# A Sinkhorn-sorted attention with a bilinear feed-forward: k and v of later batches mixed with tokens on partitions, and two edits to the start

## The chip, the cores and the metric

The kernel runs on one core of one Trainium2 chip. The metric is the device time of one execution in microseconds. The kernel before takes 245.79 us in the median of 14 runs (245.52 to 246.59).

## The reference, cut to what matters

Inputs are q, k and v of 4 batches, 8 heads, 768 tokens and 64 elements a head, an 8 x 8 matrix per head (sort_net), and the weights w_a, w_b (512 x 1536) and w_out (1536 x 512).

```python
for _ in range(5):                      # Sinkhorn
    P = exp(P - max(P, -1)); P = P / sum(P, -1); P = P / sum(P, -2)
k_sorted = einsum('bhij,bhjcd->bhicd', P, k_b)   # blocks of 96 tokens mixed by P
v_sorted = einsum('bhij,bhjcd->bhicd', P, v_b)
attn = softmax(scale * q_b @ k_sorted.T)         # within each of the 8 blocks
x = (attn @ v_sorted), heads side by side        # 3072 x 512
out = ((x @ w_a) * (x @ w_b)) @ w_out
```

## The kernel before, in words

**Tiling.** Heads are taken in pairs: 16 pairs, numbered g, four to a batch. A token's place in a tile is p * 6 + c: partition p holds six neighbouring tokens, c from 0 to 5. With 16 partitions to a block, mixing the blocks by P is one matmul with s_all, a 128 x 128 matrix per head that holds P spread over such groups of 16 (`spread`, L153). A pair's mixed k is kept as kT (64 elements of both heads on partitions, tokens along the row), its mixed v as vT in the same manner and, turned, as vs with tokens on partitions; both in three buffers (NBUF).

**Attention of a pair.** `stage_mix` (L274) makes, for k and then v, 12 matmuls of 128 columns whose weights are 64 columns wide (6 c by 2 heads), and ACT or ACT with DVE copies the result from PSUM in the order of kT or vT. For v a transpose on SP's DMA queue (L292) makes vs from vT, but for pair 4, where `turn_v` does it on TensorE. `turn_q` (L255) or `pair_q` and `stage_q` (L244, L250: a copy on Pool and a transpose on SP) make qT. `stage_scores` (L295) makes two PSUM tiles of scores, and ACT's Exp makes eT. `stage_o` (L310, through `one_o`, L226) multiplies eT by vs, and DVE divides by the row sums into xp; `to_xT` (L316) turns xp into xT by a transpose on SP's queue. The first batch does the same in two halves of four blocks with `half_mix`, `half_scores`, `half_v`, `half_o` and `half_x` (L172 to L224), all turning on TensorE.

**Feed-forward.** `ffn_ab` (L340) takes one of 12 slices of 128 hidden columns and one half of a batch's 768 tokens: four matmuls of 384 columns by w_a and four by w_b (`ab_mms`, L330), a copy by ACT (a_sb, L352) and a product by DVE into hT (L353). `ffn_out` (L368) multiplies hT by w_out in six output tiles, each in two steps of six matmuls, and `store` copies and writes one tile.

**What sets the order.** TensorE, Pool and SP run in the order of the program text; ACT and DVE do in the start (L400 to L494), and after that a scheduler places them. The start holds the Sinkhorn chain on DVE and ACT, with unused matmuls on TensorE beside it (`keep_busy`, L166; L407 and L427), then the first half of batch 0's attention. Five feed-forward tiles are begun there without their last matmul (L488 to L494), which needs x of pair 3. Then attention work is cut in units and put between feed-forward steps: `interleave` (L562) runs the second half of batch 0 with its own steps, and `paced` (L571) spreads the 12 units of batch b + 1 (`units_full`, L531) over the steps of batch b. A unit is the mix of a pair (c_), its scores (s_), or its output with to_xT (o_). c_ of pair g also copies one element of kT on Pool (gate, L540), so that Pool issues the loads of pair g + 2 (L541) after k has been mixed. Loads run on Pool's queue and change float32 to bf16. PSUM has four single banks (psF) and two double ones (psA); mix, scores and o share psA.

Of the kernel before, what the change touches and what calls it, by code (L numbers as in the profile page):

```python
# [9 lines left out]
FP32 = mybir.dt.float32  # L10
BF16 = mybir.dt.bfloat16
# [11 lines left out]
def kernel(  # L23
# [11 lines left out]
    nc = tc.nc  # L35
    P = 128
# [129 lines left out]
    def keep_busy(ps, n, cols=512):  # L166
        for _ in range(n):
            nc.tensor.matmul(ps[:, 0:cols], lhsT=warm[:, 0:P], rhs=warm[:, 0:cols],  # L168
                             start=True, stop=True)
# [33 lines left out]
    def half_v(h, hp):  # L203
        g = h * HP + hp
        vT, vs = vTs[g % NBUF], vss[g % NBUF]
        vs_ps = psF.tile([P, NBH, 2, D], BF16, tag="F", name="vs_ps")
        for i in range(NBH):
            nc.tensor.matmul(vs_ps[:, i], lhsT=vT[:, i], rhs=ident, is_transpose=True)  # L208
        nc.vector.tensor_copy(out=vs[0:BLK, 0:NBH, V0:V0 + P],
                              in_=vs_ps[0:BLK].rearrange("p i e d -> p i (e d)"))  # L210
# [7 lines left out]
    def half_x(h, hp, eng):  # L218
        xT, xp = xT_of(0), st["x", h, hp]
        xt_ps = psF.tile([P, NBH, BLK], BF16, tag="F", name="xt_ps")  # L220
        for i in range(NBH):
            nc.tensor.matmul(xt_ps[:, i, :], lhsT=xp[:, i],  # L222
                             rhs=ident[0:BLK, 0:BLK], is_transpose=True)
        copy(eng, xT[:, hp, h * HW:(h + 1) * HW].rearrange("p (i t) -> p i t", i=NBH), xt_ps)  # L224
# [25 lines left out]
    def stage_q(g):  # L250
        qT = qtp.tile([P, NCH, P], BF16, tag="qTf", name="qTf", bufs=4)
        nc.sync.dma_start_transpose(out=qT, in_=st[g, "qc"].rearrange("p c e d -> p (c e d)"))
        st[g, "qT"] = qT
# [20 lines left out]
    def stage_mix(g, what, engines):  # L274
        src2 = loaded[g][0 if what == "k" else 1]
        to = (kTs if what == "k" else vTs)[g % NBUF]
        pitch, whole = (BLK, S + PAD) if what == "k" else (P, NB * P)
        mix = psA.tile([P, 2, 512], FP32, tag="A", name="mix")
        for c in range(NCH):
            for e in range(2):  # L280
                nc.tensor.matmul(  # L281
                    mix[e * D:(e + 1) * D, c // 3, c % 3 * P:(c % 3 + 1) * P],
                    lhsT=src2[:, e, c * D:(c + 1) * D],
                    rhs=s_all[:, 2 * g + e], start=True, stop=True)
        for hf, eng in enumerate(engines):
            n = 2 // len(engines)
            for u in range(n):
                d1 = _ap(to, (hf + u) * 3 * CG, [[whole, P], [CG, 3], [pitch, NB], [1, CG]])
                s1 = _ap(mix, (hf + u) * 512, [[1024, P], [P, 3], [CG, NB], [1, CG]])
                copy(eng, d1, s1)  # L290
        if what == "v" and g > HP:
            nc.sync.dma_start_transpose(out=vss[g % NBUF][:, :, V0:V0 + P],  # L292
                                        in_=to.rearrange("p i t -> p (i t)"))

    def stage_scores(g):  # L295
        kT, qT, eT = kTs[g % NBUF], st[g, "qT"], eTs[g % NBUF]
# [33 lines left out]
    def ab_mms(pf, w_sb, b, m, t, kcs):  # L330
        for kc in kcs:
            nc.tensor.matmul(pf[:, 0:HW], lhsT=w_sb[:, kc, m * P:(m + 1) * P],  # L332
                             rhs=x_cols(b, kc, t), start=(kc == 0), stop=(kc == KA - 1))

    def hT_of(b):
        if b not in hTs:
            hTs[b] = ffp.tile([P, KO, S], BF16, tag="hT", name="hT")
        return hTs[b]

    def ffn_ab(b, m, t, begun=()):  # L340
# [58 lines left out]
    with tc.manual_schedule(engines={ET.PE, ET.Pool, ET.SP}):  # L399
        with tc.manual_schedule(engines={ET.Activation, ET.DVE}):  # L400
# [3 lines left out]
            p_rep = const.tile([BH, NB * NB, CG // 2], FP32, name="p_rep")  # L404
            pc_ps = psA.tile([P, NB, BH], FP32, tag="A", name="pc_ps")
            heat = psA.tile([P, 2, 512], FP32, tag="A", name="heat")
            keep_busy(heat[:, 0], 8)  # L407
            for it in range(5):
                nc.scalar.activation(out=p_nat, in_=p_nat, func=AF.Exp)
                if it == 2:  # L410
                    turn_q(0, "act")
                if it == 3:
                    turn_q(1, "act")
                if it == 4:
                    turn_q(2, "act")
                    turn_q(3, "act")
                if it == 2:
                    with nc.allow_low_precision("sum of one one and zeros"):
                        nc.vector.reduce_sum(
                            out=mask, in_=_ap(ident, 0, [[P, P], [1, CG], [CG, NB]]),  # L420
                            axis=AX.X)
                nc.vector.reduce_sum(out=rsum, in_=p_nat, axis=AX.X)
                nc.vector.reciprocal(out=rsum, in_=rsum)
                if it > 0:
                    nc.tensor.matmul(heat[0:NB, 1, 0:NB], lhsT=rsum, rhs=rsum,
                                     start=True, stop=True)
                    keep_busy(heat[:, 0], (0, 4, 3, 2, 4)[it])  # L427
                nc.vector.tensor_mul(out=p_nat, in0=p_nat,
                                     in1=_ap(rsum, 0, [[NB, BH], [1, NB], [0, NB]]))
                nc.vector.reduce_sum(out=csum, in_=p_nat.transpose([0, 2, 1]), axis=AX.X)  # L430
                nc.vector.reciprocal(out=csum, in_=csum)
                if it < 4:
                    nc.vector.tensor_mul(out=p_nat, in0=p_nat,
                                         in1=_ap(csum, 0, [[NB, BH], [0, NB], [1, NB]]))
                else:
                    nc.vector.tensor_mul(
                        out=p_fin.bitcast(BF16).rearrange("h (i j u) -> h i j u", i=NB, j=NB),
                        in0=_ap(p_nat, 0, [[NB * NB, BH], [NB, NB], [1, NB], [0, 2]]),
                        in1=_ap(csum, 0, [[NB, BH], [0, NB], [1, NB], [0, 2]]))
# [43 lines left out]
            half_o(0, 2)  # L483
            half_scores(0, 3)
            half_v(0, 3)
            half_x(0, 2, "act")
            half_o(0, 3)
            begun = [psF.tile([P, 512], FP32, tag="F", name="pf") for _ in range(3)]  # L488
            begun += [psA.tile([P, 2, 512], FP32, tag="A", name="two")[:, 0] for _ in range(2)]
            for n, (m, w_sb) in enumerate(((0, w_a_sb), (0, w_b_sb), (1, w_a_sb),  # L490
                                           (1, w_b_sb), (2, w_a_sb))):
                if n == 3:
                    half_x(0, 3, "act")
                ab_mms(begun[n], w_sb, 0, m, 0, range(KA - 1))  # L494


        for c in range(4, 6):
# [30 lines left out]
            us.append(lambda: half_x(1, HP - 1, "dve"))  # L528
            return us

        def units_full(b):  # L531
            g0, us = b * HP, []

            def c_(g):
                if g < 2 * HP - 2:
                    turn_q(g)
                stage_mix(g, "k", ("act",))
                stage_mix(g, "v", ("dve", "act"))
                if 2 * HP - 2 <= g < B * HP - 2:
                    nc.gpsimd.tensor_copy(out=gate, in_=kTs[g % NBUF][0:1, 0:1])  # L540
                    load_pair((g + 2) // HP, (g + 2) % HP)  # L541

            def s_(g):
                stage_scores(g)
                if g == HP:
                    turn_v(g)
                if g in (HP, HP + 1):
                    stage_q(g + 2)
                if 2 * HP <= g + 1 < B * HP:
                    pair_q(g + 1)  # L550
                    stage_q(g + 1)

            def o_(g):
                stage_o(g)
                to_xT(g)

            for u, n in ((c_, 0), (s_, 0), (c_, 1), (s_, 1), (c_, 2), (o_, 0), (s_, 2), (c_, 3),
                         (o_, 1), (s_, 3), (o_, 2), (o_, 3)):
                us.append(lambda u=u, g=g0 + n: u(g))
            return us  # L560

        def interleave(steps, units, spare, slow=0):  # L562
            n, done = len(steps), 0
# [4 lines left out]
                    units[done]()  # L568
                    done += 1

        def paced(ab, po, units, spare):  # L571
            steps = ab + po
            total = len(steps) - 2 * spare
            done = 0
            for now, step in enumerate(steps, 1):
                step()
                while done < len(units) and done * total < now * len(units):
                    units[done]()
                    done += 1

        steps = [lambda: ffn_ab(0, 0, 0, begun[0:2]), lambda: ffn_ab(0, 1, 0, begun[2:4]),
                 lambda: ffn_ab(0, 2, 0, begun[4:5])]
# [3 lines left out]
        for b in range(B):  # L586
            ab = [lambda m=m, t=t, b=b: ffn_ab(b, m, t)
                  for m in range(KO) for t in range(2) if b > 0 or t == 1]
            po = [f for c in range(NCH) for f in ffn_out(b, c)]
            paced(ab, po, units_full(b + 1) if b + 1 < B else [], 3 if b == 0 else 2)  # L590


# [28 lines left out]
```

The softmax here doesn't subtract the row's maximum and nothing guards it: scores larger than these inputs give would overflow.

## Time and profile before

| what | value |
|---|---|
| median of 14 runs | 245.79 us (245.52 to 246.59) |
| the profiled execution | 246.59 us, of which its span is 244.8 us |
| granted TensorE clock | 1.0 over the span, from 7.3 us on |
| TensorE, weight loads, DVE, ACT, Pool busy | 97%, 56%, 45%, 43%, 25% |
| DMA packets | 53929, 28.02 MB |
| share of 16 DMA engines, Pool's queue and SP's | 40.9% and 29.4% |
| transposes on SP's queue | 33: vs 11, xT 12, qTf 10 |

An engine's share is its busy time over the span. The page cuts the span in 40 slices of 6.1 us, and each digit is a busy share in tenths:

```
PE   7898999999999999999999999999999999999994
DMA  5999999987999659995783449926223310000132
```

A row of the timeline has the start and the busy time of one or of several equal instructions, in us; what stood idle before it and what ended that is in brackets. A matmul's end is modelled, so distances from start to start are the ones to read. A DMA has its issue on its queue, and its landing, which is when the last of its 16 parts is done.

### The profile page before, as it was taken

What the parts mean: (1) busy time and instruction counts of PE and PEld (TensorE: products, weight loads), DVE (VectorE), ACT (ScalarE), POOL (GpSimd) and SP (SyncE); (2) the same over time, 40 slices, a digit from 0 to 9 for tenths busy, and PEclk for the clock granted to TensorE, in tenths of its full rate; (3) what the DMA queues carried; (4) which work ended last, traced back from release to release, by engine and by line L of the source; (5) the groups of instructions that cost most, each with busy time, mean ns of one, the idle gap of its engine ahead of it and who ended that gap; (6) DMA issues with size and microseconds to landing.
All of it is one profiled execution on the core that took longest, in us unless ns stands there. A gap on an engine that the chain in (4) does not pass through costs nothing.

```text
span 244.8 us, 5499 instructions
## 1 busy us (share of the span) xinstructions
PE 237.8 (97%) x2246; PEld 137.2 (56%) x2246; DVE 109.2 (45%) x258; ACT 104.5 (43%) x204; POOL 61.4 (25%) x88
## 2 busy tenths in 40 slices
PE   7898999999999999999999999999999999999994
PEld 2475666566645466666654466666654466565442
DVE  6675466554536144464625134454525244444110
ACT  3664764566630065646440065646430133333001
POOL 8876478612240033250500053110000000000000
PEclk9999999999999999999999999999999999999999
DMA  5999999987999659995783449926223310000132
GB/s 80 201 199 197 198 199 201 203 115 78 159 129 220 137 99 132 160 138 81 109 141 118 120 94 125 168 46 67 43 79 118 117 46 0 0 3 1 43 129 86
DMA packets 53929, 28.02 MB, mean 114 GB/s; under 512 B 30736, under 2 KB 50960, under 8 KB 53904
## 3 DMA queue, kind: packets, MB, share of 16 engines
q0 software_dynamic: 20944, 14.16, 40.9%
q1 hardware_dynamic: 32816, 13.45, 29.4%
q8 instruction: 17, 0.28, 0.5%
q14 instruction: 8, 0.07, 0.1%
q10 hardware_dynamic: 144, 0.07, 0.1%
HBM read 28.32 MB, written 6.29 MB: 141 GB/s over the span
## 4 chain that ended last, share of the span: by engine, by line
PE 94%; DVE 3%; ACT 1%; issue 1%
PE pf L332 51%; PE po L377 24%; PE mix L281 4%; PE o_ps L231 3%; PE sc L302 2%; PE heat L168 2%; PE mixh L180 2%; PE po L362 1%; PE vs_ps L208 1%; PE sc L195 1%; PE xt_ps L222 1%; PE q_ps L260 1%; PE two L332 1%; DVE xp L237 1%; DVE o_sb L164 0%
## 5 line engine op out<-in xcount | busy, mean ns | idle before, releaser
L353 DVE TENSOR_TENSOR hT<-a_sb,pf 128x384 bf16<-128x384 bf16 x95 | 52.6, 554 | 73.8 <-PE pf L332 46.4
L332 PE MATMUL pf<-xT,w_a_sb 128*128 128x384 bf16 x380 | 77.9, 326 | 0.0
L332 PE MATMUL pf<-xT,w_b_sb 128*128 128x384 bf16 x380 | 77.5, 326 | 0.0
L352 ACT CAST a_sb<-pf 128x384 bf16<-128x384 f32 x95 | 45.5, 479 | 60.9 <-PE pf L332 41.3
L377 PE MATMUL po<-w_out_sb,hT 128*128 128x512 bf16 x276 | 61.9, 379 | 0.0
L332 PEld LDWEIGHTS <-w_b_sb 128*128 128x128 bf16 x384 | 37.5, 98 | 24.6
L332 PEld LDWEIGHTS <-w_a_sb 128*128 128x128 bf16 x384 | 34.9, 98 | 22.3
L377 PEld LDWEIGHTS <-hT 128*128 128x128 bf16 x276 | 26.3, 98 | 30.0
L162 ACT COPY o_sb<-po 128x512 f32<-128x512 f32 (+1 forms) x13 | 7.5, 578 | 46.8 <-PE po L377 45.2
L164 DVE COPY o_sb<-po 128x512 f32<-128x512 f32 (+1 forms) x12 | 7.9, 656 | 35.2 <-PE po L377 26.3
L307 ACT ACTIVATE eT<-sc 96x768 bf16<-96x768 f32 x24 | 18.1, 802 | 6.8 <-PE sc L302 6.8
L540 POOL COPY gate<-kT 1x1 bf16<-1x1 bf16 x8 | 1.4, 180 | 76.1 <-ACT kT L162 76.1
L237 DVE TENSOR_TENSOR xp<-o_ps,rec 96x512 bf16<-96x512 f32 x24 | 15.9, 684 | 0.6 <-DVE rec L235 0.2
L162 ACT CAST kT<-mix 128x384 bf16<-128x384 f32 x24 | 10.3, 482 | 7.9 <-PE mix L281 7.9
L95 POOL DMA_DIRECT2D k<-in_k_dram x16 | 11.6, 722 | 5.1 <-PE pf L332 2.3
L95 POOL DMA_DIRECT2D v<-in_v_dram x16 | 11.5, 719 | 2.6 <-DMA w_b_sb<-in_moe_w_b_dram 0.9
L231 PEld LDWEIGHTS <-eT 96*128 96x128 bf16 x256 | 10.3, 97 | 3.1 <-DVE xp L237 0.6
L235 DVE RECIPROCAL rec<-o_ps 96x8 f32<-96x8 f32 x32 | 5.6, 189 | 13.8 <-PE o_ps L231 13.8
L231 PE MATMUL o_ps<-vs,eT 96*128 96x65 bf16 x256 | 11.3, 193 | 0.2 <-DVE xp L237 0.2
L246 POOL COPY qc<-q 128x768 bf16<-128x768 bf16 x10 | 8.4, 837 | 8.1 <-DMA q<-in_q_dram 8.1
L168 PE MATMUL heat<-warm 128*128 128x512 bf16 x21 | 7.9, 523 | 1.3 <-DVE warm L77 1.3
L95 POOL DMA_DIRECT2D q<-in_q_dram x12 | 8.6, 718 | 1.4 <-DMA w_b_sb<-in_moe_w_b_dram 0.6
(80 smaller groups left out, 154.5 us busy)
## 6 DMA issues: line engine op xcount, KB each, us to landing
out_dram<-o_sb SPq DMA_DIRECT2D x17, 256.0 KB, 2.0
k<-in_k_dram POOLq DMA_DIRECT2D x16, 192.0 KB, 5.4
v<-in_v_dram POOLq DMA_DIRECT2D x16, 192.0 KB, 7.0
q<-in_q_dram POOLq DMA_DIRECT2D x12, 192.0 KB, 7.1
w_a_sb<-in_moe_w_a_dram POOLq DMA_DIRECT2D x6, 256.0 KB, 10.1
w_b_sb<-in_moe_w_b_dram POOLq DMA_DIRECT2D x6, 256.0 KB, 10.5
w_out_sb<-in_moe_w_out_dram POOLq DMA_DIRECT2D x3, 512.0 KB, 12.1
out_dram<-o_sb SPq DMA_DIRECT2D x12, 128.0 KB, 2.7
```

Source lines behind the costliest of these rows:

```text
L95: nc.gpsimd.dma_start(out=to, in_=_ap(t, base, [[W, P], [S * D, 2], [1, W]]))
L162: nc.scalar.copy(out=out, in_=in_)
L168: nc.tensor.matmul(ps[:, 0:cols], lhsT=warm[:, 0:P], rhs=warm[:, 0:cols], start=True, stop=True)
L231: nc.tensor.matmul(o_ps[:, e, i * (D + 1):(i + 1) * (D + 1)], lhsT=eT[:, hf, e, i * BLK:i * BLK + P], rhs=vs[0:BLK, i0 + i, V0 - 1 + e * ( ...
L237: nc.vector.tensor_tensor(out=_ap(xp, i0 * 2 * D, [[nxp * 2 * D, BLK], [D, 2], [2 * D, NBH], [1, D]]), in0=_ap(o_ps, 1, [[1024, BLK], [511 ...
L246: nc.gpsimd.tensor_copy(out=qc.rearrange("p c e d -> p e c d"), in_=loaded[g][2].rearrange("p e (c d) -> p e c d", c=NCH))
L281: nc.tensor.matmul(mix[e * D:(e + 1) * D, c // 3, c % 3 * P:(c % 3 + 1) * P], lhsT=src2[:, e, c * D:(c + 1) * D], rhs=s_all[:, 2 * g + e], ...
L307: nc.scalar.activation(out=eT[:, hf, :, 0:HB], in_=sc[0:BLK, :, 0:HB], func=AF.Exp, scale=float(scale))
L332: nc.tensor.matmul(pf[:, 0:HW], lhsT=w_sb[:, kc, m * P:(m + 1) * P], rhs=x_cols(b, kc, t), start=(kc == 0), stop=(kc == KA - 1))
L352: nc.scalar.copy(out=a_sb, in_=pf[:, 0:HW])
L353: nc.vector.tensor_mul(out=hT[:, m, t * HW:(t + 1) * HW], in0=a_sb, in1=ab[1][:, 0:HW])
L377: nc.tensor.matmul(held["po"], lhsT=hTs[b][:, m, c * P:(c + 1) * P], rhs=w_out_sb[:, m, :], start=(m == 0), stop=(m == KO - 1))
```

## The change

It has these parts.
- The unused matmuls of the Sinkhorn chain are 128 columns wide, four for each one of 512.
- The first feed-forward tile is begun earlier: its first two matmuls stand between half_v(0, 3) and half_x(0, 2).
- Pairs 5 to 15 mix k and v in `stage_kv`: s_all is the weights and k or v the moving operand, 384 columns, so mixed tokens stand on partitions (nat). ACT, or DVE and ACT, copies it, a transpose on SP turns it (turned), and `order_kv` copies it on Pool to kT and vT in block order. `return_v` then issues the transpose from vT to vs that stage_mix issued before.
- The units' order is written out in `plan`. order_kv stands one unit after the mix and return_v two; the loads of pair g + 2 stand one unit after the mix, or three if g is 8 or 12, and without the gate copy. pair_q and stage_q move to the mix unit. Mixes of pairs 9 and 13 are done a batch earlier than before, ahead of the last step of the batch (`last`), and that of pair 8 moves into batch 0.
- hT has one buffer in place of two.

```diff
+    def stage_kv(g):
+        for n, (what, engines) in enumerate((("k", ("act",)), ("v", ("dve", "act")))):
+            src2 = loaded[g][n]
+            mix = psA.tile([P, 2, 512], FP32, tag="A", name="mix")
+            for e in range(2):
+                nc.tensor.matmul(mix[:, e, 0:W], lhsT=s_all[:, 2 * g + e], rhs=src2[:, e],
+                                 start=True, stop=True)
+            nat = att.tile([P, NCH, 2, D], BF16, tag="nat", name="nat")
+            step = 2 // len(engines)
+            for u, eng in enumerate(engines):
+                copy(eng, nat[:, :, u * step:(u + 1) * step].rearrange("p c e d -> p e c d"),
+                     mix[:, u * step:(u + 1) * step, 0:W].rearrange("p e (c d) -> p e c d", c=NCH))
+            turned = att.tile([P, NCH, P], BF16, tag="turned", name="turned")
+            nc.sync.dma_start_transpose(out=turned, in_=nat.rearrange("p c e d -> p (c e d)"))
+            st[g, what, "nat"], st[g, what] = nat, turned
+
+    def order_kv(g):
+        for what, to in (("k", kTs[g % NBUF][:, 0:S].rearrange("p (i c t) -> p c i t", i=NB, c=NCH)),
+                         ("v", vTs[g % NBUF][:, :, 0:BLK].rearrange("p i (c t) -> p c i t", c=NCH))):
+            nc.gpsimd.tensor_copy(out=to, in_=st[g, what].rearrange("p c (i t) -> p c i t", i=NB))
+
+    def return_v(g):
+        nc.sync.dma_start_transpose(out=vss[g % NBUF][:, :, V0:V0 + P],
+                                    in_=vTs[g % NBUF].rearrange("p i t -> p (i t)"))
...
-            hTs[b] = ffp.tile([P, KO, S], BF16, tag="hT", name="hT")
+            hTs[b] = ffp.tile([P, KO, S], BF16, tag="hT", name="hT", bufs=1)
...
-            keep_busy(heat[:, 0], 8)
+            keep_busy(heat[:, 0], 32, P)
...
-                    keep_busy(heat[:, 0], (0, 4, 3, 2, 4)[it])
+                    keep_busy(heat[:, 0], (0, 16, 12, 8, 16)[it], P)
...
+            begun = [psF.tile([P, 512], FP32, tag="F", name="pf")]
+            ab_mms(begun[0], w_a_sb, 0, 0, 0, range(2))
             half_x(0, 2, "act")
             half_o(0, 3)
-            begun = [psF.tile([P, 512], FP32, tag="F", name="pf") for _ in range(3)]
+            begun += [psF.tile([P, 512], FP32, tag="F", name="pf") for _ in range(2)]
...
-                ab_mms(begun[n], w_sb, 0, m, 0, range(KA - 1))
+                ab_mms(begun[n], w_sb, 0, m, 0, range(0 if n else 2, KA - 1))
...
+        def c_(g):
+            if g > HP:
+                stage_kv(g)
+                if g >= 2 * HP - 2:
+                    if g >= 2 * HP:
+                        pair_q(g)
+                    stage_q(g)
+            else:
                 stage_mix(g, "k", ("act",))
                 stage_mix(g, "v", ("dve", "act"))
...
+        plan(0, "c4", "c5", "s4", "c6", "s5", "o4", "c7", "s6", "o5", "c8", "s7", "o6", "o7", "c9")
+        plan(1, "s8", "c10", "s9", "o8", "c11", "s10", "o9", "c12", "s11", "o10", "o11", "c13")
+        plan(2, "s12", "c14", "s13", "o12", "c15", "s14", "o13", "s15", "o14", "o15")
+        after = [[] for _ in seq]
+        for n, (b, u, g) in enumerate(seq):
+            if u is c_ and g > HP:
+                after[n + 1].append(lambda g=g: order_kv(g))
+                after[n + 3 if g % HP == 0 else n + 1].append(lambda g=g: load_later(g))
+                after[n + 2].append(lambda g=g: return_v(g))
...
-        def paced(ab, po, units, spare):
+        def paced(ab, po, units, spare, last):
             steps = ab + po
             total = len(steps) - 2 * spare
-            done = 0
+            main, done = len(units) - last, 0
             for now, step in enumerate(steps, 1):
                 step()
-                while done < len(units) and done * total < now * len(units):
+                while done < main and done * total < now * main:
                     units[done]()
                     done += 1
+                if now == len(steps) - 1 and last:
+                    units[main]()
...
-            paced(ab, po, units_full(b + 1) if b + 1 < B else [], 3 if b == 0 else 2)
+            paced(ab, po, units[b], 3 if b == 0 else 2, 1 if b < B - 2 else 0)
```

More of the change, by code (lines that the diff above doesn't have):

```diff
@@ L290, in stage_mix @@
                 copy(eng, d1, s1)
-        if what == "v" and g > HP:
-            nc.sync.dma_start_transpose(out=vss[g % NBUF][:, :, V0:V0 + P],
-                                        in_=to.rearrange("p i t -> p (i t)"))
+    def stage_kv(g):
[20 more added lines that the diff above has]
+                                    in_=vTs[g % NBUF].rearrange("p i t -> p (i t)"))
     def stage_scores(g):
@@ L529, in units_half @@
             return us
[L531 to L536, printed above, removed]
+        def c_(g):
[6 more added lines that the diff above has]
+            else:
                 stage_mix(g, "k", ("act",))
                 stage_mix(g, "v", ("dve", "act"))
[L539 to L560, printed above, removed]
@@ new lines, in s_, with o_, load_later, plan @@
+        def s_(g):
+            stage_scores(g)
+            if g == HP:
+                turn_v(g)
+        def o_(g):
+            stage_o(g)
+            to_xT(g)
+        def load_later(g):
+            if 2 * HP - 2 <= g < B * HP - 2:
+                load_pair((g + 2) // HP, (g + 2) % HP)
+        units = [[] for _ in range(B)]
+        seq = []
+        def plan(b, *names):
+            for name in names:
+                seq.append((b, {"c": c_, "s": s_, "o": o_}[name[0]], int(name[1:])))
@@ L562, in interleave, with unit @@
+        def unit(u, g, then):
+            if u is c_ and g < 2 * HP - 2:
+                turn_q(g)
+            u(g)
+            for f in then:
+                f()
+        for (b, u, g), then in zip(seq, after):
+            units[b].append(lambda u=u, g=g, then=then: unit(u, g, then))
         def interleave(steps, units, spare, slow=0):
```

## The prediction

> **What bounds the kernel now.** I read the shares of busy time first, then the chain that ended last, then the timeline of TensorE around one unit of attention work, then the rows and landings of the DMA queues.
>
> ```profile
> span 244.8 us, 5499 instructions
> PE 237.8 (97%) x2246; PEld 137.2 (56%) x2246; DVE 109.2 (45%) x258; ACT 104.5 (43%) x204; POOL 61.4 (25%) x88
> ...
> PE 94%; DVE 3%; ACT 1%; issue 1%
> PE pf L332 51%; PE po L377 24%; PE mix L281 4%; PE o_ps L231 3%; PE sc L302 2%; PE heat L168 2%; PE mixh L180 2%; PE po L362 1%; PE vs_ps L208 1%; PE sc L195 1%; PE xt_ps L222 1%; PE q_ps L260 1%; PE two L332 1%; DVE xp L237 1%; DVE o_sb L164 0%
> ```
>
> The reader is to see that from about 22 us on TensorE is the bound: a matmul that goes is a gain, and a wait of TensorE on anything is a loss of its full length. The timeline of TensorE at one mix of a later batch (start, busy us, what):
>
> ```profile
> 93.43 0.81 PE L332 MATMUL pf<-xT,w_a_sb 128*128 128x384 bf16 x4
> 94.08 0.81 PE L332 MATMUL pf<-xT,w_b_sb 128*128 128x384 bf16 x4
> 94.83 0.53 PE L281 MATMUL mix<-s_all,k 128*64 128x128 bf16 x12
> 95.19 0.50 PE L281 MATMUL mix<-s_all,v 128*64 128x128 bf16 x12
> 95.62 0.82 PE L332 MATMUL pf<-xT,w_a_sb 128*128 128x384 bf16 x4
> 96.28 0.81 PE L332 MATMUL pf<-xT,w_b_sb 128*128 128x384 bf16 x4
> ```
>
> Read start to start, since ends are modelled. Four pf take 0.65 (93.43 to 94.08), but 0.75 where the next is a mix (94.08 to 94.83); k takes 0.36, v 0.43, and the four pf after it 0.66. So a pair's mix costs 0.10 + 0.36 + 0.43 + 0.01 = 0.90 us, of which only 12 x 2 x 0.030 = 0.72 is its own pace. The rest lies where 128*64 tiles begin and end. No such step stands around o_ps (107.48 to 107.97, pf before and after at 0.65), whose weights are 128 columns wide.
>
> The transposes on SP's queue, their time to landing by line, and the Pool and SP rows of the first batch:
>
> ```profile
> vs<-vT SPq DMA_TRANSPOSE x11, 6.5
> ```
>
> ```profile
> 59.71 0.77 POOL L95 DMA_DIRECT2D k<-in_k_dram  x1 [0.32 <-PE pf L332]
> 60.47 0.72 POOL L95 DMA_DIRECT2D v<-in_v_dram  x1
> 61.18 0.72 POOL L95 DMA_DIRECT2D q<-in_q_dram  x1
> ```
>
> ```profile
> 60.10 1.23 SPq L292 DMA_TRANSPOSE vs<-vT  x1
> 62.50 1.22 SPq L318 DMA_TRANSPOSE xT<-xp  x1
> 67.24 1.23 SPq L292 DMA_TRANSPOSE vs<-vT  x1
> ```
>
> By the landing records of the trace these three loads took 3.83, 7.61 and 8.26 us, and the two transposes beside them 7.06 and 7.50. A transpose with no load beside it lands in 2.8 to 3.2. The vs of 67.24, again beside three loads, took 7.31 and landed at 74.55; its reader o_ps starts at 75.57. The first batch is near that edge already.
>
> [...] the chain has 0.81 us of "issue" at 18.21, with an instruction packet at 16.74.
>
> **The change, part by part.** Unused matmuls (L168): 8 of 512 columns become 32 of 128, and 4, 3, 2, 4 become 16, 12, 8, 16. Columns stay equal. Until the granted clock rises, at 7.3 us in the trace, the 512s start 427 ns apart. No row shows full weights with 128 columns at that clock; [...] After it, 4 x 57 (vs_ps pace) against 216 adds 0.04 for 12 pieces, beside the ACT copy of qT, which ends 0.3 ahead of its next Exp. I take 0. Bounds: -0.7 if the full clock comes earlier (the qT copy at 7.59 to 8.39 then no longer stands ahead of the Exp); +1.3 if each piece costs the 147 ns of its weight load until the clock rises. The pieces put 126 more rows ahead of the mixes, [...] I take its 0.8 as moved, 0 net, with 0.5 to either side.
>
> Part of an output tile: two pf matmuls (2 x 0.162) go ahead of half_x(0,2). TensorE waits there: vs_ps starts at 20.82, needs 0.23, the next starts at 21.65 for DVE's xph. 0.6 us of idle hold 0.32; the xT of pairs 0 and 1 is there at 20.76. What is late next is xph of pair 3, done at 23.35, with TensorE arriving at 23.36. Gain 0.31.
>
> k and v with tokens on partitions, pairs 5 to 15: 24 matmuls become 4 of 384 columns with 128-column weights, the shape of pf: 4 x 0.1625 = 0.65. No tile mode changes. Ten pairs gain 0.90 - 0.65 = 0.25 each: 2.46. Pair 5 keeps turn_q (128*64) in front and gains 0.04. Sum on TensorE: 2.46 + 0.04 + 0.31 = 2.81. The copies: one ACT copy of 768 (0.80, the qT row) for two of 0.48; v as before. DVE and ACT are 45 and 43% busy, so nothing.
>
> What is added: per pair two more transposes on SP (22 in all, 1.2 of SP each, up to 2.2 back to back: the qTf of 56.03) and two Pool copies of 768. The qc row, also 768, takes 0.84; [...] Upper bound 1.5, at the rate of the spread row (2.0 for 1024). I take 0.84. k now reaches kT through copy, transpose and Pool; v through these and its old transpose back. Behind Pool's wait for v stand the next loads; behind SP's stand everything queued. The gate copy goes. hT in one buffer: its first writer follows the last po of the old batch on TensorE anyway, 0.
>
> In batches 1 and 2 scores come four units (over 15 us) after their mix, except pair 9 at some 10: I take 0. In batch 0 it is tight. The new units in place, with steps of 1.30, scores 0.55, o 0.49, mix 0.65, give due times without waits: mix 6 done 55.1, scores 6 at 63.35, mix 7 done 62.0, mix 8 at 68.3, scores 7 at 70.25, o 7 at 75.2.
> - Pair 6: k copied at 55.8, transposes issued 55.8 to 59.5. A pair issued at 54.75 and 56.03 landed at 59.35 and 59.93; so k, v, q at about 60.4, 61.3, 62. Pool done at 62.2. In time.
> - Loads of pair 8 follow that on Pool: 62.5 in place of 59.7. At 7.6, v lands at 70.8; mix 8 wants it at 68.6. Wait 2.2.
> - Pair 7: k, v, q issued 63.4 to 67.1 behind two or three transposes and beside these loads. The xT of 62.50 landed 0.56 after the last load; so q at 72.8. Scores 7, now due 72.45, wait 0.3.
> - v 7 is in vT at about 72.9; its transpose back goes out at 73.0, beside the loads of pair 9. 6.5 (the median) gives 79.5. o 7, now due 77.8, waits 1.7.
> Sum of waits 4.2, from 0 to 6.5 (every transpose of a train at 2.2). Pool and SP run late by the same, and the batch's end absorbs it.
>
> Against the profiled execution (span 244.8 and 1.8 around it, 246.59): 246.59 - 2.8 + 4.2 = 248.0. It is the slowest of the runs; the median is 245.79, so 247.2.
>
> **Rivals.** No or short waits: the DMA engines take the two extra transposes of a pair in their gaps. For it: the DMA digits of slices 8 to 10 are 8, 7, 9, and the k load of a trio lands in 3.8. Against: the landings above. With 0.9 of waits, 245.8 - 2.8 + 0.9 = 243.9; with none and an early clock 242.3. It decides on whether vs of pair 7 lands within 2 us of o 7's due time: waits below 2.3 make it faster.
>
> Balance: waits of 2.3 to 3.3 eat the gain: 245.8. For it: loads or transposes each a little quicker than the rows beside a full trio.
>
> More waits: the late first batch reaches batch 1. xT of pair 7 is issued behind vs 8 and the next batch's first tile reads it; a further 2 gives 249.2. The same time comes if the change doesn't do what it says and the 4 matmuls cost 0.90 a pair: 247.2 + 2.5 = 249.7.
>
> **How the numbers follow.** Forecast 247.2 (246.3 to 248.4): 0.46. More waits: 0.09. Balance: 0.11. Faster, about 243.9: 0.34. A measurement of this kernel can tell 0.2%, 0.5 us. So faster 0.34, same 0.11, slower 0.55. The range leaves out some 0.1 on either side: 243.3 to 248.9.
>
> **What would show it.** Right: pf before and after the new mix at 0.65, the mix at 0.65; TensorE idle ahead of mix, sc or o_ps between 66 and 80 us; vs landings over 6 us. Wrong: TensorE without gaps there (then faster), a wait at the scores of batches 1 or 2, or a first q_ps much later than 6.8.

## The result and the profile after

The changed kernel takes 252.01 us in the median of 10 runs (248.94 to 253.72), the kernel before 245.81 in 47 runs beside them: a ratio of 1.0219 (95% interval 1.0201 to 1.0236). The ratio is of fast runs alone (two of the ten, 253.33 and 253.72, are not among them), and so it is not the 1.025 of the two medians. The prediction was 247.2 with a range up to 248.9. Its direction holds; the loss is 6.2 us between the medians (5.4 by the ratio) in place of 1.4. The profiled execution after took 251.38 us, 4.79 more than the one before.

First the page of the kernel after: span, busy time, two rows of the 40 slices (6.2 us each), and the chain that ended last.

```profile
span 249.6 us, 5246 instructions
...
PE 237.6 (95%) x2089; PEld 139.2 (56%) x2089; DVE 109.1 (44%) x258; ACT 104.1 (42%) x193; POOL 77.4 (31%) x102
...
PE   7899999989969959999999999999999999999995
...
PEclk9999999999979998999999999999999999999999
...
PE 81%; DMA 11%; DVE 4%; ACT 1%; POOL 1%; issue 1%; POOLq 0%
```

TensorE is busy for 237.6 us, against 237.8 before, but DMA now holds 11% of the chain. After the start, all the dips lie in slices 9 to 16, the second half of batch 0 and the start of batch 1. From 97 us on there is none. And the second row has something that the kernel before does not: the granted clock falls twice in mid-kernel. The clock records of the trace put it at 0.5 from 72.18 to 75.59 and from 92.66 to 96.07, 3.41 us each.

The new mix in a later batch, in the timeline of TensorE (start, busy us, what):

```profile
144.83 0.81 PE L399 MATMUL po<-w_out_sb,hT 128*128 128x512 bf16 x3
145.48 0.49 PE L297 MATMUL mix<-k,s_all 128*128 128x384 bf16 x2
145.80 0.49 PE L297 MATMUL mix<-v,s_all 128*128 128x384 bf16 x2
146.13 1.46 PE L399 MATMUL po<-w_out_sb,hT 128*128 128x512 bf16 x6
```

Start to start, k takes 0.32 and v 0.33, and the three po ahead take 3 x 0.216 with nothing on top: 0.65 a pair, as predicted. Now the two largest waits of TensorE, with the rows that run at the halved clock behind each. The brackets give the idle time and what ended it.

```profile
68.58 1.46 PE L399 MATMUL po<-w_out_sb,hT 128*128 128x512 bf16 x6
72.04 0.74 PE L324 MATMUL sc<-qTf,kT 64*128 64x96 bf16 x16 [2.01 <-DMA qTf<-qc]
72.72 4.17 PE L399 MATMUL po<-w_out_sb,hT 128*128 128x512 bf16 x12
76.72 0.66 PE L231 MATMUL o_ps<-vs,eT 96*128 96x65 bf16 x16
...
89.40 0.49 PE L354 MATMUL pf<-xT,w_a_sb 128*128 128x384 bf16 x2
91.66 0.32 PE L354 MATMUL pf<-xT,w_a_sb 128*128 128x384 bf16 x1 [1.77 <-DMA xT<-xp]
92.99 0.48 PE L354 MATMUL pf<-xT,w_a_sb 128*128 128x384 bf16 x1 [1.00 <-DMA xT<-xp]
93.26 1.48 PE L354 MATMUL pf<-xT,w_b_sb 128*128 128x384 bf16 x4
94.68 0.82 PE L324 MATMUL sc<-qTf,kT 64*128 64x96 bf16 x16
95.44 1.12 PE L354 MATMUL pf<-xT,w_a_sb 128*128 128x384 bf16 x4
96.39 0.81 PE L354 MATMUL pf<-xT,w_b_sb 128*128 128x384 bf16 x4
```

At 72.04 the scores of pair 7 wait for q of pair 7. At 89.40 batch 1 begins: its first two matmuls run, the third waits for xT of pair 6 (landed 91.62), the fourth for xT of pair 7 (landed 92.95). Start to start, the four take 3.86 us (89.40 to 93.26) in place of 0.65, so 3.2 are lost. Both xT come from SP's queue. Its timeline (start, time that SP spent issuing):

```profile
72.42 1.25 SPq L314 DMA_TRANSPOSE vs<-vT  x1
73.76 3.33 SPq L305 DMA_TRANSPOSE turned<-nat  x2
77.18 3.54 SPq L252 DMA_TRANSPOSE qTf<-qc  x1
80.81 3.34 SPq L412 DMA_DIRECT2D out_dram<-o_sb  x4
84.24 1.41 SPq L340 DMA_TRANSPOSE xT<-xp  x1
85.75 1.72 SPq L314 DMA_TRANSPOSE vs<-vT  x1
87.56 2.84 SPq L340 DMA_TRANSPOSE xT<-xp  x1
90.49 3.75 SPq L412 DMA_DIRECT2D out_dram<-o_sb  x6
```

Each row begins 0.1 after the one ahead of it has ended: SP has no free moment from 72.42 to 94.2. The 11 issues from vs of pair 7 to xT of pair 7 take 18.0 us. One transpose, q of pair 8, holds SP for 3.54. The study turns on these rows.

Taking the two profiled executions apart by stage, with the start of batch 1's first tile (85.48 before, 89.40 after) as the mark:

| term | us |
|---|---|
| start, up to 42 us | -1.63 |
| mix of pairs 5 to 15 | -2.54 |
| TensorE's waits in batch 0, start to start: scores 5 0.7, mix 8 0.2, scores 7 2.1, o 7 0.7; less 0.6 that stood before (scores 7 0.2, o 7 0.4) | +3.1 |
| wait for xT of pairs 6 and 7 at batch 1 | +3.2 |
| clock at half, twice: rows behind the two waits, start to start, 1.65 and 1.3 longer than at the full clock | +2.9 |
| end of the kernel | -0.3 |
| sum (measured 4.79) | +4.7 |

This adds up, but it is arithmetic, not yet cause: e7 and e8 below show that some of these terms would come back elsewhere if they were removed.

### The profile page after: what moved, and what is told of

The parts are those of the page before. It is cut to its first block, busy times and chain, and to the rows that moved or that the text cites. A ratio compares the mean times of both kernels' runs of the same rounds, so it can differ in the third digit from the quotient of the medians.

```text
span 249.6 us, 5246 instructions
## 1 busy us (share of the span) xinstructions
PE 237.6 (95%) x2089; PEld 139.2 (56%) x2089; DVE 109.1 (44%) x258; ACT 104.1 (42%) x193; POOL 77.4 (31%) x102
## 3 DMA queue, kind: packets, MB, share of 16 engines
q0 software_dynamic: 20944, 14.16, 40.6%
q1 hardware_dynamic: 50416, 17.78, 37.5%
## 4 chain that ended last, share of the span: by engine, by line
PE 81%; DMA 11%; DVE 4%; ACT 1%; POOL 1%; issue 1%; POOLq 0%
PE pf L354 47%; PE po L399 21%; DMA turned<-nat 5%; PE o_ps L231 3%; DMA vs<-vT 3%; DMA xT<-xp 2%; PE mix L297 2%; PE sc L324 2%; PE mixh L180 2%; PE po L384 1%; PE vs_ps L208 1%; PE xt_ps L222 1%; PE sc L195 1%; DMA p_nat<-in_sort_net_dram 1%; PE two L354 1%
## 5 line engine op out<-in xcount | busy, mean ns | idle before, releaser
L354 PE MATMUL pf<-xT,w_a_sb 128*128 128x384 bf16 x380 | 78.7, 328 | 3.0 <-DMA xT<-xp 2.8
L399 PE MATMUL po<-w_out_sb,hT 128*128 128x512 bf16 x276 | 63.3, 385 | 0.0
L354 PEld LDWEIGHTS <-w_a_sb 128*128 128x128 bf16 x384 | 35.8, 98 | 24.8 <-issue 2.3
L311 POOL COPY kT<-turned 128x768 bf16<-128x768 bf16 x11 | 9.1, 829 | 77.4 <-DMA turned<-nat 57.3
L162 ACT CAST nat<-mix 128x768 bf16<-128x768 f32 (+1 forms) x22 | 14.1, 639 | 8.9 <-PE mix L297 6.9
L311 POOL COPY vT<-turned 128x768 bf16<-128x768 bf16 x11 | 9.1, 830 | 4.3 <-DMA turned<-nat 4.3
L164 DVE CAST nat<-mix 128x384 bf16<-128x384 f32 x11 | 6.1, 557 | 7.5 <-PE mix L297 7.3
```

The costliest lines, as they stand in the source:

```text
L162: nc.scalar.copy(out=out, in_=in_)
L164: nc.vector.tensor_copy(out=out, in_=in_)
L311: nc.gpsimd.tensor_copy(out=to, in_=st[g, what].rearrange("p c (i t) -> p c i t", i=NB))
L399: nc.tensor.matmul(held["po"], lhsT=hTs[b][:, m, c * P:(c + 1) * P], rhs=w_out_sb[:, m, :], start=(m == 0), stop=(m == KO - 1))
```

## The experiments

My theory after the result: the added transposes share the 16 DMA engines with the loads of pairs 8 to 10 (on the page after, Pool's queue takes 40.6% of the 16 engines' span and SP's 37.5%), so SP's queue falls behind; TensorE waits; and each long wait halves the clock once. The rivals: the train of transposes on one queue is too long by itself, loads or not; or the shifted start makes the waits; or the mix saves nothing. The ratios are to the kernel before, run beside each; its medians were 245.8 to 246.0.

**e1: the pieces alone.** The kernel before, with

```diff
-            keep_busy(heat[:, 0], 8)
+            keep_busy(heat[:, 0], 32, P)
...
-                    keep_busy(heat[:, 0], (0, 4, 3, 2, 4)[it])
+                    keep_busy(heat[:, 0], (0, 16, 12, 8, 16)[it], P)
```

> The kernel before with one part of the change, the unused matmuls in pieces of 128 columns. Theory: these pieces alone bring the start's gain, that is the granted clock rises about 3.4 us earlier (3.9 in place of 7.3) so that the Sinkhorn chain ends 0.7 earlier, and the wait of 0.8 for an instruction block at 18.2 goes because the block now falls due inside the chain, where TensorE has time. Time 244.2, ratio 0.9935. Rival, the earlier clock is chance or belongs to another part: 245.8, ratio 1.000, with the wait of 0.8 still at about 18.

Measured: 245.1 us (9 runs), ratio 0.9965 (0.9952 to 0.9977), so 0.86 less. Half of the theory holds. The wait at L195 is gone; this is the timeline of TensorE in e1, where the eight scores of L195 now run through:

```profile
16.95 0.41 PE L231 MATMUL o_ps<-vs,eT 96*128 96x65 bf16 x8
17.29 0.34 PE L195 MATMUL sc<-qT,kT 64*128 64x96 bf16 x8
17.57 0.40 PE L208 MATMUL vs_ps<-ident,vT 128*128 128x128 bf16 x4
```

The kernel before has a break of 0.81 us between the sixth and the seventh of them. The first packet of the instruction queue q8 during the run comes at 10.86 in e1 (16.74 before), inside the Sinkhorn chain. The kernel after has its own at 10.86 too, and TensorE runs unused matmuls there (10.30 to 11.37). That TensorE waited for this packet is inferred from the times; the next packet of e1, at 17.68, brought no such wait. The other half is not borne out. The clock's first rise came at 5.5 in e1 and between 3.9 and 7.2 in all ten profiled executions with the pieces; with 512 columns it came at 4.8, 6.0 and 7.3. The ranges overlap, so nothing here shows that the pieces bring it forward.

**e2: the begun tile alone.** The kernel before, with

```diff
+            begun = [psF.tile([P, 512], FP32, tag="F", name="pf")]
+            ab_mms(begun[0], w_a_sb, 0, 0, 0, range(2))
             half_x(0, 2, "act")
...
-                ab_mms(begun[n], w_sb, 0, m, 0, range(KA - 1))
+                ab_mms(begun[n], w_sb, 0, m, 0, range(0 if n else 2, KA - 1))
```

> The kernel before with the begun output tile alone moved. Theory from the trace after: the two matmuls that go in find an idle stretch, but the next ones then wait for the x of pair 2, so the gain is taken back: 245.8, ratio 1.000. The prediction's own term: 0.31 less, 245.5, ratio 0.9987.

Measured: 246.23 (12 runs), ratio 1.0005 (0.9993 to 1.0017), which leaves the 0.9987 of a gain of 0.31 just outside. The theory holds. The timeline of TensorE in e2:

```profile
20.53 0.49 PE L332 MATMUL pf<-xT,w_a_sb 128*128 128x384 bf16 x2
21.13 0.35 PE L222 MATMUL xt_ps<-ident,xph 96*128 96x96 bf16 x4
21.46 0.40 PE L231 MATMUL o_ps<-vs,eT 96*128 96x65 bf16 x8
22.04 0.32 PE L332 MATMUL pf<-xT,w_a_sb 128*128 128x384 bf16 x1 [0.18 <-ACT xT L162]
```

The two matmuls of 20.53 sit in the idle stretch, as meant. The next tile matmul needs x of pair 2, which xt_ps has only just turned and ACT must still copy. Before, the two matmuls that are now gone covered that copy.

**e3: the new mix without the two edits to the start.** The kernel after with e1's and e2's edits undone.

> The kernel after with the old unused matmuls and the old place of the begun tile, so only the new mix of k and v and its plan. Theory, the slowdown comes wholly from the waits of the first batch and what the clock does after them: the start's 1.6 is lost and the rest is as after, 253.2 (ratio 1.030), with waits of over 1.5 ahead of scores 7 and ahead of batch 1's first tile, and the granted clock at half for some 3 us after each. Rival, the earlier start of the changed kernel itself makes the waits (loads fall due later against TensorE): 250 or less, ratio 1.017.

Measured: 252.23 (4 runs, 249.88 to 253.26), ratio 1.0235 (1.0178 to 1.0291). The same waits stand in the same places (2.8 ahead of scores 7, 3.2 at batch 1's first tile), with the clock at half from 74.27 and from 94.75, 3.41 each. So the new mix and its plan alone make the slowdown. The lost start of 1.6 shows between the profiled executions (253.26 against 251.38) but not between medians of runs that spread over 3 us; these four runs can't settle its size.

**e4: the new mix only from pair 9 on.** Pairs 5 to 8 as before, in the changed plan, with q turned in the mix unit (`FIRST = 9`):

```diff
-            if g > HP:
+            if g >= FIRST:
                 stage_kv(g)
...
+                if g >= 2 * HP - 2:
+                    nc.gpsimd.tensor_copy(out=gate, in_=kTs[g % NBUF][0:1, 0:1])
+                    load_later(g)
+            if g >= 2 * HP - 2:
+                if g >= 2 * HP:
+                    pair_q(g)
+                stage_q(g)
```

> The kernel after, but pairs 5 to 8 are mixed as before; k and v stand with tokens on partitions from pair 9 on. Theory, the whole slowdown is the first batch's waits, and the new mix saves 0.25 a pair where nothing waits: 245.8 - 1.6 (start) - 7 x 0.25 = 242.4, ratio 0.986, no gap on TensorE after 22 us. Rival 1, the saving of the mix is not there: 244.2, ratio 0.9935. Rival 2, the waits move on to pair 9 and batch 1 because of what SP and Pool carry: over 245, ratio 1.00 or more, with a gap of over 1 us between 85 and 125 us.

Measured: 247.44 (20 runs, 245.0 to 251.8), ratio 1.0039 (1.0017 to 1.0061). Neither 242.4 nor a wait where rival 2 put it. TensorE in e4:

```profile
62.10 0.81 PE L358 MATMUL pf<-xT,w_b_sb 128*128 128x384 bf16 x4
65.85 0.52 PE L328 MATMUL sc<-qTf,kT 64*128 64x96 bf16 x16 [2.94 <-DMA qTf<-qc]
```

The wait is my own making: in this plan q of pair 6 is turned at 56.78, in the midst of the loads of pair 8 (issued 55.11 to 57.32), and lands 8.94 us later. The kernel before turned it at 56.03, ahead of the loads, in 3.90. So one transpose put beside three loads made such a wait with no new mix near it: a part of the waits in batch 0 can come from where the new plan puts q. Batch 1's first tile waits for nothing in e4: xT of pairs 6 and 7 went out at 82.18 and 83.54 and landed by 86.50, and the loads of pair 10, issued from 74.52 on, had landed at 82.92. The run also prices the clock. Of its 20 runs, 6 had a mean clock of 1.0 (245.0 to 246.7, mean 245.9), and 11 had 0.993, which is one stretch of 3.41 us at half in some 245 (the profiled execution after, with two, has 0.986), and took 246.8 to 248.5 (mean 247.7): about 1.8 us for one stretch.

**e5: the first batch wholly as before, the new mix from pair 9.** e4, with q turned in s_ and the old order of batch 0, pairs 8 and 9 mixed ahead of its last step:

```diff
-        plan(0, "c4", "c5", "s4", "c6", "s5", "o4", "c7", "s6", "o5", "c8", "s7", "o6", "o7", "c9")
+        plan(0, "c4", "s4", "c5", "s5", "c6", "o4", "s6", "c7", "o5", "s7", "o6", "o7", "c8", "c9")
```

> The kernel after, with the whole first batch as in the kernel before (its units in the old order, pairs 5 to 8 mixed in the old way, q turned where it was, loads behind the gate copy), pairs 8 and 9 mixed ahead of its last step, and the new mix and plan from pair 9 on. Theory: the waits belong to the first batch alone, where the loads run beside the new transposes; the new mix saves 0.25 for each of 7 pairs and the start's fetch stall of 0.8 goes with the pieces: 246.0 - 0.9 - 1.75 = 243.4, ratio 0.989, granted clock 1.0 throughout and no gap of TensorE over 0.4 after 22 us. Rival, the waits move on to pair 9 and the first units of batch 1: 245 to 248, with a gap of over 1 us between 85 and 105 us.

Measured: 245.7 (16 runs, 245.1 to 249.03), ratio 1.000 (0.9982 to 1.0018). The rival wins, but its two waits can be read off:

```profile
84.30 0.48 PE L301 MATMUL mix<-k,s_all 128*128 128x384 bf16 x2 [0.62 <-ACT kT L163]
...
92.95 0.50 PE L301 MATMUL mix<-v,s_all 128*128 128x384 bf16 x2 [1.54 <-DMA v<-in_v_dram]
```

The mixes of pairs 8 and 9 stand back to back and share two PSUM tiles (0.7 lost, start to start), and the mix of pair 10 comes ahead of its load (1.7). The 243.4 of the theory with these two, 243.4 + 0.7 + 1.7 = 245.8, is near the 245.7 measured. Both are matters of order, which e9 takes up.

**e6: the kernel after without the loads of pairs 8 to 10.**

```diff
+            if 8 <= b * HP + hp <= 10:
+                nc.vector.memset(to, 0.5)
+            else:
                 nc.gpsimd.dma_start(out=to, in_=_ap(t, base, [[W, P], [S * D, 2], [1, W]]))
```

> The kernel after, but k, v and q of pairs 8, 9 and 10 are not loaded: VectorE fills their tiles with a constant, so the outputs of those three pairs leave out their inputs. Everything else, all 33 + 22 transposes too, is as after. Theory 1, the waits come from transposes and loads sharing the 16 DMA engines: transposes land in 2.7 to 3.5 as where no load runs, SP issues each in 1.2 to 2.2, no wait over 0.3 at scores 7, o 7 and batch 1's first tile, no halved clock, and 252.0 - 6.8 - 2.9 = 242.3. Theory 2, the chain of added transposes on one queue (issued one after the other, each behind the one before) makes the waits by itself: scores 7 and batch 1's first tile still wait over 1 us each and the time stays above 247.

Measured: 243.37 (4 runs), ratio 0.9895 (0.9876 to 0.9914). This decides between the first two theories: with all the transposes still there, no wait of TensorE on a DMA is left after 45 us. Transposes from nat land in 2.9 in the median (4.2 in the kernel after). Of the 1.1 above the 242.3 expected, two waits of TensorE for VectorE near 39 and 43 us (0.5 and 0.8, start to start) stand where VectorE fills the tiles. SP's queue in e6, from vs of pair 7 to xT of pair 7:

```profile
70.39 1.25 SPq L317 DMA_TRANSPOSE vs<-vT  x1
71.73 2.58 SPq L308 DMA_TRANSPOSE turned<-nat  x2
74.41 1.24 SPq L255 DMA_TRANSPOSE qTf<-qc  x1
75.74 2.46 SPq L415 DMA_DIRECT2D out_dram<-o_sb  x4
78.29 1.29 SPq L343 DMA_TRANSPOSE xT<-xp  x1
79.68 1.39 SPq L317 DMA_TRANSPOSE vs<-vT  x1
81.16 1.26 SPq L343 DMA_TRANSPOSE xT<-xp  x1
```

The same 11 issues take 12.0 us in place of 18.0. So the loads lengthened not only the flight of a transpose (2.9 against 4.2) but also the time that SP needed to hand it over (1.24 against 3.54 for q of pair 8).

**e7: what stands ahead of xT of pair 7 moved behind it.** The kernel after, with

```diff
-                after[n + 3 if g % HP == 0 else n + 1].append(lambda g=g: load_later(g))
-                after[n + 2].append(lambda g=g: return_v(g))
+                after[n + (4 if g == 2 * HP else 3 if g % HP == 0 else 1)].append(lambda g=g: load_later(g))
+                after[n + (3 if g == 2 * HP else 2)].append(lambda g=g: return_v(g))
```

> The kernel after, with the transpose back of v of pair 8 issued behind xT of pair 7 in place of ahead of it, and the loads of pair 10 one unit later. Theory: batch 1's first tile waits for xT of pair 7 because these stand ahead of it on SP and beside it on the DMA engines; xT 7 is issued at about 85.8 and lands by 89.5, the wait of 3.2 and the halved clock after it (1.4) go, and 252.0 - 4.6 = 247.4. Rival: SP is late already when it reaches xT of pair 6 (84.2 in the kernel after), so xT 7 lands after 91 all the same and at most 1.5 is gained: 250.5 or more.

Measured: 251.85 (4 runs, 250.32 to 252.56), ratio 1.0231 (1.0191 to 1.0271). The rival holds. xT of pair 7 goes out at 85.14 in place of 87.56 and lands at 92.92 in place of 92.95. TensorE in e7:

```profile
90.01 0.32 PE L354 MATMUL pf<-xT,w_a_sb 128*128 128x384 bf16 x1 [0.52 <-DMA xT<-xp]
92.96 0.32 PE L354 MATMUL pf<-xT,w_a_sb 128*128 128x384 bf16 x1 [2.63 <-DMA xT<-xp]
```

The loads of pair 10 did not move in time: Pool reached them at 83.31 (83.05 in the kernel after), since it was held up by the late transposes of pair 8 and not by the unit that they stand in. Issued 2.42 us earlier into the same crowd, the transpose landed at the same moment. So the moment at which SP issues this one transpose doesn't set batch 1's start; what is in flight beside it counts. In both kernels the loads of pair 10 are: they landed at 91.56 in the kernel after and at 92.41 in e7. In the kernel before they went out from 88.91 on, behind batch 1's start at 85.48. The new plan, which moves the mix of pair 8 into batch 0, brings them ahead of that start. Their own share is not separated, since e7 left them where they were.

**e8: the waits filled.** The kernel after, with unused matmuls in the waits (stage_scores shown; one_o and ffn_ab have the like):

```diff
+    FILL = {("s", 7): 9, ("o", 7): 2, ("b", 1): 13}
...
             sc = psA.tile([P, 2, 512], FP32, tag="A", name="sc")
+            if hf == 0:
+                keep_busy(sc[:, 0], FILL.get(("s", g), 0))
```

> The kernel after, with unused matmuls of 512 columns in the three waits (9 ahead of scores 7, 2 ahead of o 7, 13 ahead of batch 1's first tile, 216 ns each, written to the PSUM tile that the real matmuls then overwrite). The waits stay, TensorE doesn't idle in them. Theory: the halved clock follows from the idle time, so it stays at 1.0 and 2.9 is gained; 252.0 - 2.9 = 249.1, and less spread than after's 248.9 to 253.7. Rival: the clock halves for another reason [...], it still drops to 0.5 for 3.4 us, and the time is 252 or more.

Measured: 250.27 (4 runs, 249.64 to 250.46), ratio 1.0171 (1.0147 to 1.0194). The clock stays at 1.0 in all four runs, and they lie within 0.8 us (4.8 in the ten runs of the kernel after). So the halving followed from idle time here: without it there was none in four runs. The one run of the kernel after whose clock stayed at 1.0 took 250.24, the same as e8. But the gain is 1.7 between the medians (1.2 by the ratios), not 2.9. TensorE in e8:

```profile
88.32 2.75 PE L169 MATMUL pf<-warm 128*128 128x512 bf16 x12
91.13 0.49 PE L359 MATMUL pf<-xT,w_a_sb 128*128 128x384 bf16 x2
91.83 0.32 PE L359 MATMUL pf<-xT,w_a_sb 128*128 128x384 bf16 x1 [0.21 <-DMA xT<-xp]
93.40 0.32 PE L359 MATMUL pf<-xT,w_a_sb 128*128 128x384 bf16 x1 [1.25 <-DMA xT<-xp]
```

TensorE reaches batch 1 at 88.32, 1.1 before the kernel after (89.40), because the first halved stretch is gone. It then waits for xT of pair 7 until 93.40 all the same (92.99 after). Only the second halved stretch, behind that wait, is a gain. e7 and e8 together: batch 1's start is set by when the transposes of SP's queue land, and what TensorE lost earlier in batch 0 is absorbed there.

**e9: e5 with its order mended.** Batch 1 has o 8 ahead of the mix of pair 10, and mixes 8 and 9 stand one step apart (an edit of `paced`, not shown):

```diff
-        plan(1, "s8", "c10", "s9", "o8", "c11", "s10", "o9", "c12", "s11", "o10", "o11", "c13")
+        plan(1, "s8", "o8", "c10", "s9", "c11", "o9", "s10", "c12", "o10", "s11", "o11", "c13")
```

> The run before it with the first batch kept, e5, with two changes of order: in batch 1 the output of pair 8 comes ahead of the mix of pair 10 (so this mix, which waited 1.7 for v of pair 10, falls due one unit later), and the mixes of pairs 8 and 9 at the end of batch 0 stand one step apart. Theory: e5's 245.7 is the saving of 0.25 a pair with two waits of 0.5 and 1.7 on top; without them 243.4 to 243.6, ratio 0.990. Rival: each shift makes the next wait (mix 11 for its v, scores 10 for kT, at 0.5 to 2 us), 244.5 to 246, ratio 0.995 to 1.00.

Measured: 242.94 (4 runs, 242.85 to 243.21), ratio 0.9883 (0.9867 to 0.9899): faster than both kernels. The rows of e9:

```profile
span 241.2 us, 5381 instructions
...
PE   7999999999999999999999999999999999999995
...
PEclk9999999999999999999999999999999999999999
```

No slice dips. Yet the transposes of pair 9 at 84.92 and 86.33 land in 9.69 and 8.80, longer than any in the kernel after. They have landed by 95.13, and their first reader on TensorE, scores 9, comes at 99.01, so nobody waits.

**e10: the new mix for pairs 13 to 15 alone,** the first two batches in their old order (`FIRST = 13`; c12 and c13 ahead of batch 1's last two steps).

> The first two batches in the order and manner of the kernel before, the mix of pair 12 (old) and 13 (new) ahead of batch 1's last two steps, and the new mix for pairs 13 to 15 alone, where few loads are left; pieces and begun tile as in the kernel after. Theory: no wait anywhere, 246.0 - 0.86 (fetch stall) - 3 x 0.25 = 244.4, ratio 0.9935. Rival: waits at the scores of pair 13 or batch 2's first tiles of 0.5 or more, 244.9 to 246.

Measured: 243.94 (5 runs), ratio 0.9921 (0.9905 to 0.9937), without a wait. The saving goes with the number of pairs: 3 pairs here, 7 in e9. The four pairs between are worth (0.9921 - 0.9883) x 245.8 = 0.93 us, 0.23 each.

**e11: e9's order with the old mix** (`FIRST = 16`).

> The fast version e9 with its order of units kept and all pairs mixed in the old way, so that the mix alone differs between the two (q's transposes stand with the scores of the pair before, as in the kernel before). Theory: the mix saves 0.25 for each of the 7 pairs 9 to 15, and the order by itself nothing: 245.8 - 0.86 (fetch stall) = 244.9, ratio 0.9965, some 1.75 to 2.0 above e9's 242.94. Rival: part of e9's gain comes from its order (mixes 8 and 9 ahead of batch 0's end, q earlier): 244.2 or less, ratio under 0.994.

Measured: 245.22 (23 runs), ratio 0.9972 (0.9962 to 0.9981). The order by itself brings nothing beyond e1's 0.86. Between e11 and e9 lie (0.9972 - 0.9883) x 245.9 = 2.2 us for 7 pairs, 0.31 each. The 0.25 from the timeline is somewhat less. A wait of 1 us at o 8, which e11's profiled execution has and e9's hasn't, may be part of the difference; that execution took 247.2, the longest of the 23, so how often the wait comes is not known.

## Why the prediction was wrong

It had the mechanism, added transposes landing late beside loads, and sized the loss at 1.4 us in place of 6.2. It followed the lateness to the first readers and not past them. Step by step:

- **The mix, 0.25 a pair.** Right: 0.65 in the trace, and e9 to e11.
- **Added waits in batch 0, 4.2.** They came to 3.1, with the parts shifted, so that the sum is not far off owes something to luck. Mix 8 waited 0.2 and not 2.2. I let k, v and q of pair 6 land at 60.4 to 62; they landed at 57.3, 58.6 and 60.0, and the loads of pair 8 went out at 59.56 and not at 62.5. Pool after:

```profile
57.44 0.83 POOL L311 COPY kT<-turned 128x768 bf16<-128x768 bf16 x1 [0.76 <-DMA turned<-nat]
58.79 0.83 POOL L311 COPY vT<-turned 128x768 bf16<-128x768 bf16 x1 [0.52 <-DMA turned<-nat]
59.56 0.76 POOL L95 DMA_DIRECT2D k<-in_k_dram  x1
```

Three transposes in a row with no load beside them took 2.74, 2.83 and 2.83: these did not slow each other down. The Pool copies took 0.83 each; the 0.84 taken for them was an estimate from the qc row. What mix 8 didn't wait, scores 7 did: 2.1 for q of pair 7, which landed at 71.91 (72.8 predicted). vs of pair 7 landed at 79.06 (79.5 predicted). Scores 5, which the prediction passed over, waited 0.7: k of pair 5 was turned beside the last load of w_out and took 5.93.

- **"Pool and SP run late by the same, and the batch's end absorbs it."** This is the step that failed. The landings in batch 0 were near (within 1 us for q and v of pair 7); what they do to the queue behind them was not followed to the end. SP is busy without a break from 72.42, and xT of pairs 6 and 7, issued at 84.24 and 87.56 beside the loads of pair 10, land at 91.62 and 92.95, where TensorE asks for them from 89.7: 3.2 us. The prediction had this only as a rival with 0.09 and 2 us, and it didn't price the loads of pair 10, which the new plan puts beside both xT. e7 and e8 show the reverse of the sentence: the end of the batch absorbs TensorE's waits, and the lateness of SP's transposes is what reaches batch 1.
- **The clock, not in the sum at all.** A second term that was missing: 2.9 us by the account above, some 1.2 to 1.7 of it recoverable by itself (e8). In the clock records after, each drop lasts 3.41, and the first, at 72.18, comes 68.27 us, 20 times as long, after the first rise at 3.91. The 3.41 us ahead of the two drops held 2.2 and 2.8 us of idle time of TensorE. Naming the waits without this price made the long ones too cheap.
- **The begun tile, -0.31.** It was 0. I took xph of pair 3 for what is late next; it is ACT's copy of x of pair 2 (e2).
- **The pieces, 0, with the 0.8 of the wait at L195 "moved, 0 net".** That it would come back elsewhere in the start was my estimate, which no trace had shown. It did not: -0.86 (e1; the expectations call this wait the fetch stall). In the trace after, pieces of 128 columns start 107 ns apart before the first rise, so four take 428 against the 427 of one of 512. No effect of the pieces on the clock's first rise, for which the bound of -0.7 stood, is seen.
- **No waits at scores in batches 1 and 2.** Right; scores 8 took 0.3 longer in the clock's second halved stretch, and that is all.

From 248.0 (profiled): start -1.3, waits of batch 0 -1.1, batch 1's wait +3.2, clock +2.9, end -0.3 gives 251.4, against 251.38.

Open: how the slowdown splits between SP's queue, Pool's waiting behind it and the loads of pair 10 that the new plan brings ahead of batch 1 was not separated. No run took the new transposes away and kept both the plan and the times of its loads. e4 comes nearest, with the old mix up to pair 8: batch 1's first tile waits for nothing there, but its loads of pair 10 go out from 74.52 on and not from 83.05.

## What to carry to other kernels

When a change adds DMA work to a queue, follow that queue to its end, past the first reader that waits, and count how long the issuing engine is held and who stands behind it. Where the order changes too, look up which loads now run beside which transposes. A saving on the bound engine is safe where the longer path has slack in time (in e9 some 15 us from mix 9 to scores 9), so move the readers away before the work is added. Where the bound is TensorE, price a long wait at its length and, at risk, a halved stretch of clock after it: here 1.3 to 1.8 us, behind 2.2 to 3.2 us of idle time within one stretch of 3.41.

## What the runs showed of the hardware that was not expected

- The halved clock came and went in whole stretches of 3.413 us. Between one change of the granted clock and the next lie 68.267, 3.413, 17.067, 3.413 and 153.600 us in the kernel after (20, 1, 5, 1 and 45 stretches) and 238.933 in the kernel before (70). Counting stretches from the first rise, and idle time from start-to-start distances, five with 2.2, 2.4, 2.8, 2.8 and 3.2 us idle (kernels after, e3, e4) were each followed by one at 0.5. Ten with 1.0 to 1.8 idle (e3, e5, e7, e8) were not. In e7 waits of 2.6 and 3.5 (the latter 0.7 and 2.8) fell across the borders of stretches and cost no clock: its profiled execution has a mean of 0.999. The first rise, from which they are counted, came anywhere from 3.9 to 7.2 in the ten profiled executions with the pieces. That can explain only a part of the spread of 4.8 us in the kernel after, against 1.1 before: a run with a mean clock of 0.993, which is one halved stretch, took 248.94, and the one at 1.0 took 250.24.
- SP was held longest where loads ran beside its transposes: up to 3.8 us for one in the kernel after and 5.1 in e3 (at 106.01), against 1.2 to 1.3 for most where no load ran (2.4 once, in e6 at 65.25).
- A transpose alone, or in a train of its like, mostly landed in 2.7 to 3.3 (one train of e6 took 4.0 to 4.9); beside three loads mostly in 5.4 to 9.7, and beside six, in e11, in 9.9 and 10.6.
